# Attention with a low-rank mixer and an MLP on one core: squares, casts and roots of the first five head groups put on other engines and other places in the queues

## The chip, the cores and the metric

The kernel runs on one core of a Trainium2 chip. The metric is the device time of the run in microseconds (us). All times of the profile are from one profiled execution; its clock starts with the first instruction.

## The reference

```python
# q, k, v: (8, 12, 448, 64); g_q, g_k: (64,); U: (448, 32); V: (32, 448)
# w_ch1: (768, 3072); w_ch2: (3072, 768); all float32
rms(x, g) = x / sqrt(mean(x * x, -1) + 1e-6) * g
scores    = rms(q, g_q) @ rms(k, g_k).T / sqrt(64)
attn      = softmax(scores)                       # per batch and head, 448 x 448
x         = (attn @ v), heads side by side        # (8, 448, 768)
u         = x + (x.T @ U @ V).T                   # mixes the 448 tokens through rank 32
out       = u + relu(u @ w_ch1) @ w_ch2           # (8, 448, 768)
```

## The kernel before, in words

**Groups and pairs.** The 96 heads are taken in 24 groups of four heads (three groups to a batch), and each group in two pairs. "Group 0" is the first. A pair is named by batch and number; pairs 0 and 1 belong to group 0, pairs 2 and 3 to group 1, and so on.

**A group's preparation.** Its q, k and v are loaded as float32 (`load_qk`, `load_v`, issued by SyncE). `squares` (line 133) squares q or k, on ScalarE or, where an engine is given, on GpSimd. `sums` (line 158) adds up each row of 64 on VectorE. `roots` (line 161) makes 1/rms from both sums with two short ScalarE instructions (a logarithm, line 165, and an exponential, line 166). `scale` (line 168) multiplies q and k by it and writes bf16 `qn` and `kp`; for most groups both on GpSimd. `turn` (line 339) transposes seven 128x128 blocks on TensorE into PSUM, and `take_q` and `take_k` (lines 347 and 356) copy the result to SBUF as `qT` and `kz`. `values` (line 194) casts v to bf16 in three instructions, one for `va` and two for `vl`. Groups from 6 on are transposed by DMA instead and are not touched by the change. Group 0 is cut into two parts (`PARTS`) so that its chain starts early: `squares_part`, `sums_part`, `scale_part` (line 152).

**A pair's attention.** `Sc(b, pr, r)` for r = 0 to 3 (line 390) makes the transposed scores of two 128-key blocks (for r = 3 of one) in one of two PSUM buffers `sc`, and ScalarE writes their exponentials to `E`. `V(b, pr, half)` (line 401) multiplies `E` by `vl` and `va`; VectorE divides by the sum (`r`, line 419, and `x`, line 420).

**Mixer and MLP.** For batch 0 `prep_u` casts U to `Ub` and `Uz`, `prep_v` casts V, `mix_t0` and `mix` make `uT`, and `mix_rows` (matmul `pm`, line 482, and VectorE's addition, line 490) makes u by rows. `up` (line 496; matmuls line 500, relu line 502) and `down` (line 519; matmuls line 526) are the MLP. `up_part` begins the first two of the 24 columns of `up` ahead of the others.

**The order.** Nothing is scheduled by a tool (`manual_schedule`): each engine runs its instructions in the order in which Python emits them, and semaphores make it wait for others. The front is emitted by the lines from 693 on. After it stands the list `att` of attention steps, each with a cost. For batch 0 it holds `Sc` and, behind each, what the dictionary `extra` names; then come the last V of batch 0, the mixer, and the two `up_part`; then the turning of group 3; then the steps of the later pairs. The loop at the end merges `att` with the list `mlp`: an attention step is taken when the costs of those taken so far are not past `due`. Steps of cost 0 go with the step before them, and `lambda: None` steps only spend cost, so they put off what follows.

**Filler.** `keep_busy(n)` issues n matmuls of 128 columns whose result nobody reads.

```python
        (0, 2): scales(1) + [(0, squares, (2, 1, pool)), (0, keep_busy, (8,))],
...
    squares(1, 0)
    fill_mixer()
    squares(2, 0, nc.gpsimd, ...)
    values(0)
    turn(0, 0)
    keep_busy(14)
```

Of the kernel before, what the change touches and what calls it, by code (L numbers as in the profile page):

```python
# [24 lines left out]
def kernel(  # L25
# [13 lines left out]
    nc = tc.nc  # L39
    B, H, S, D = q.shape  # L40
    dm = H * D
    dh = moe_w_ch1.shape[1]
    rank = moe_U.shape[1]
# [5 lines left out]
    R = S - SM  # L49
# [3 lines left out]
    NW = len(WIN[0])  # L53
    D1 = D + 1
# [26 lines left out]
    NM = 4 * NJ  # L81
# [18 lines left out]
    def by_c(t):  # L100
        return t.rearrange("p (c j) d -> p c j d", c=2)
# [31 lines left out]
    def squares(gi, i, eng=None, sq=None):  # L133
        if sq is None:
            sq = normp.tile([P, 2 * NT, D], FP32, name="sq", tag="sq")
        sqs[(gi, i)] = sq
        if eng is None:
            nc.scalar.activation(sq, staged[gi][i], AF.Square)
        else:
            eng.tensor_mul(sq, staged[gi][i], staged[gi][i])  # L140
# [11 lines left out]
    def scale_part(i, lo, hi, eng):  # L152
        eng.tensor_tensor(
            normed[0][i].rearrange("p j c d -> p c j d")[:, :, lo:hi, :], by_c(staged[0][i])[:, :, lo:hi, :],
            rss[0][:, i].rearrange("p (c j) -> p c j ()", c=2)[:, :, lo:hi, :].to_broadcast([P, 2, hi - lo, D]),
            ALU.mult)

    def sums(gi, i):
        nc.vector.tensor_reduce(ssqs[gi][:, i, :], sqs.pop((gi, i)), AX, ALU.add)  # L159
# [31 lines left out]
                rs[:, c, :2 * NJ].rearrange("p (i t) o -> p i t o", i=2).to_broadcast([P, 2, NJ, D]), ALU.mult)  # L191
            nc.gpsimd.tensor_tensor(rest, src[:, c, 2 * NJ], rs[:, c, 2 * NJ].to_broadcast([P, D]), ALU.mult)

    def values(gi):
        tv, va, vl = staged[gi][2], *normed[gi][2:]
        nc.gpsimd.tensor_copy(va[:, :, :D], tv[:, :NM, :])  # L196
        for e in range(2):
            nc.gpsimd.tensor_copy(vl[e * R:(e + 1) * R, :, e * D1:e * D1 + D], tv[e * R:(e + 1) * R, NM:, :])

    def scale_all(gi):  # L200
        roots(gi)
# [14 lines left out]
    PARTS = ((0, 4), (4, NT))  # L216
# [15 lines left out]
    def keep_busy(n):  # L232
        t = ps.tile([P, P], FP32, name="busy", tag="ps")
        for i in range(n):
            nc.tensor.matmul(t, ident, ident, start=True, stop=True)
# [53 lines left out]
    Ub = consts.tile([P, NJ + 2, rank], BF16)  # L289
    first = xp.tile([P, NW, dm], BF16, name="x", tag="x")  # L290
    Uf = first[:, 2, :2 * (NJ + 2) * rank].bitcast(FP32).rearrange("p (j r) -> p j r", r=rank)
# [26 lines left out]
    Uz = first[:, 0, :NW * P].rearrange("p (j r) -> p j r", r=P)  # L318
    tz = first[:, 1, :]

    def prep_u():
        nc.vector.tensor_copy(Ub, Uf)
        nc.vector.tensor_copy(Uz[:, :, :rank], Uf[:, :NW, :])  # L323

    tb_bufs = [consts.tile([P, 2 * P], BF16, name=f"tb{i}") for i in range(2)]

    def fill_mixer():
        nc.gpsimd.memset(Uz, 0.0)
        for t in tb_bufs:
            nc.gpsimd.memset(t, 0.0)  # L330
# [16 lines left out]
    def take_q(gi, a, scalar=False):  # L347
        qT = q_bufs[gi % 2][:, a]
        dst, src = qT.rearrange("p (j r) -> p j r", r=R), pts[(gi, 0)][:, :, a, :]
        if scalar:  # L350
            nc.scalar.mul(dst, src, gg[:, 0:1])
        else:
            nc.vector.tensor_scalar(dst, src, gg[:, 0:1], None, ALU.mult)
        qk[(gi, a)] = [qT]

    def take_k(gi, a):
        src = pts[(gi, 1)][:, :, a, :]
        kz = kz_bufs[gi % 2][:, a]
        nc.vector.tensor_copy(kz[0:D, :S].rearrange("p (j r) -> p j r", r=R), src[0:D])
        nc.vector.tensor_copy(kz[D:P, S:S + R], src[D:P, 2 * NJ])  # L360
        nc.vector.tensor_copy(kz[D:P, S + R:].rearrange("p (j r) -> p j r", r=R), src[D:P, :2 * NJ])
        qk[(gi, a)].append(kz)
# [183 lines left out]
    att = []  # L546

    def add_att(cost, f, *a):
        att.append((cost, f, a))
# [9 lines left out]
    def V2(i, half):  # L559
        return (0.55, V, (*pairs[i], half))  # L560

    pool = nc.gpsimd

    def scales(gi):
        return [(0, roots, (gi,)), (0, scale, (gi, 0, pool)), (0, scale, (gi, 1, pool))]

    def turns(gi):
# [1 line left out]

    extra = {  # L570
        (0, 0): [(0, keep_busy, (8,))],
        (0, 1): [(0, keep_busy, (8,))],
        (0, 2): scales(1) + [(0, squares, (2, 1, pool)), (0, keep_busy, (8,))],
        (0, 3): [(0, keep_busy, (8,))],
        (1, 1): [V2(0, 0)],
        (1, 2): [(0.4, turn, (1, 0)), (0, take_q, (1, 0)), (0, take_q, (1, 1))],
        (1, 3): [(0.4, turn, (1, 1)), (0, take_k, (1, 0)), V2(0, 1), (0, take_k, (1, 1)), (0, sums, (2, 1)),
                 (0, values, (1,)), (0, load, (4,)), (0, weights, (1,))],
        (2, 1): scales(2) + [(0, weights, (1,)), V2(1, 0)],
        (2, 3): [V2(1, 1), (0, prep_u, ())],  # L580
        (3, 1): [V2(2, 0)],
        (3, 2): turns(2),
        (3, 3): [V2(2, 1), (0, take_k, (2, 1)), (0, squares, (3, 0, pool)), (0, values, (2,)), (0, load, (5,)),
                 (0, weights, (1,)), (0, prep_v, (0, 1)), (0, squares, (3, 1, pool)), (0, weights, (1,))],
        (4, 0): [V2(3, 0)],
        (4, 1): [V2(3, 1), (0, sums, (3, 0))],
        (5, 0): [(0.9, mix_t0, (0, 512))],
# [4 lines left out]
    for i in range(NPAIR):  # L592
        for r in range(4):
            add_att(0.38, Sc, *pairs[i], r)
            att.extend(extra.get((i, r), []))
    att.extend([V2(5, 0), V2(5, 1), (0.39, mix, (0, 2, True)), (0.39, mix, (0, 3, True)), (0.57, up_part, (0, 0, 0, 3)),
                (0.2, mix_t0, (640, dm)), (0.39, mix, (0, 4, True)), (0.57, up_part, (0, 1, 0, 3)),
                (0.39, mix, (0, 5)), (0.19, up_part, (0, 0, 3, 4)), (0.19, up_part, (0, 1, 3, 4)),
                (0, sums, (3, 1))])
    first_done = len(att)  # L600

    att.extend([(0.6, lambda: None, ()), *scales(3)[:2], (0, scale, (3, 1, nc.vector)), (0, values, (3,)), (0.9, lambda: None, ()),
                (0.4, turn, (3, 0)), (0.4, turn, (3, 1)), (0, take_q, (3, 0)), (0, take_q, (3, 1)),
                (0, take_k, (3, 0)), (0, take_k, (3, 1)), (0.3, lambda: None, ())])

    for i, (b, pr) in enumerate(pairs):
        if b == 0:
            continue
        gi, a = divmod(i, 2)
        more = gi + 1 < len(groups)  # L610
        by_dma = gi + 1 >= DMA_FROM
        soon = gi + 2 < len(groups)

        if pr == 0 and b > 1:
            add_att(0.55, V, *pairs[i - 1], 0)
            add_att(0.55, V, *pairs[i - 1], 1)
        add_att(0.38, Sc, b, pr, 0)
        if i == 2 * DMA_FROM - 2:
            add_att(0.0, load, DMA_FROM + 1)
        if a == 0 and by_dma and gi + 1 < len(groups):  # L620
            add_att(0.0, scale_all, gi + 1)
        if b == 1 and pr == 0:
            add_att(0.4, lambda: None)
        if a == 0 and not by_dma:
            add_att(0.0, squares, gi + 1, 0, nc.gpsimd)
            add_att(0.0, squares, gi + 1, 1, nc.gpsimd)
            if gi + 2 >= DMA_FROM:
                add_att(0.0, load, gi + 2)
        add_att(0.38, Sc, b, pr, 1)
        if pr != 0:  # L630
            add_att(0.55, V, *pairs[i - 1], 0)
        if a == 1 and more and not by_dma:
            add_att(0.39, T, gi + 1, 0)
        if a == 1 and soon and gi + 2 >= DMA_FROM:
            add_att(0.0, squares, gi + 2, 0)
            add_att(0.0, squares, gi + 2, 1)
        add_att(0.38, Sc, b, pr, 2)
        if a == 0 and not by_dma:
            add_att(0.0, sums, gi + 1, 0)
            add_att(0.0, sums, gi + 1, 1)  # L640
        if a == 0 and more and by_dma:
            add_att(0.0, turn_dma, gi + 1)
            add_att(0.0, take_dma, gi + 1)
            if gi + 1 == DMA_FROM:
                add_att(0.0, weights, 2)
            if gi + 3 < len(groups):
                add_att(0.0, load, gi + 3)
        if a == 1 and more and not by_dma:
            add_att(0.39, T, gi + 1, 1)
        add_att(0.19, Sc, b, pr, 3)  # L650
        if a == 0 and not by_dma:
            add_att(0.0, scale_all, gi + 1)
        if pr != 0:
            add_att(0.55, V, *pairs[i - 1], 1)
        if a == 1 and soon and gi + 2 >= DMA_FROM:
            add_att(0.0, sums, gi + 2, 0)
            add_att(0.0, sums, gi + 2, 1)
# [35 lines left out]
    a_, b_ = PARTS  # L693
# [11 lines left out]
    roots(0, 1, 2)  # L705
    pg = prep_gains()
    keep_busy(10)
    nc.vector.tensor_copy(gg, pg)
    for part in PARTS:
        scale_part(1, *part, nc.vector)  # L710
    squares(1, 0)
    fill_mixer()
    squares(2, 0, nc.gpsimd,
            uT.rearrange("p k c -> p (k c)")[:, :4 * NT * D].bitcast(FP32).rearrange("p (j d) -> p j d", d=D))
    values(0)
    turn(0, 0)
    keep_busy(14)
    take_q(0, 0, True)
    take_q(0, 1, True)
    squares(1, 1)  # L720
    turn(0, 1)
    take_k(0, 0)
    sums(1, 0)
    sums(1, 1)
    take_k(0, 1)
    sums(2, 0)
    stage_tiles(3)
    load_qk(3, 0)
# [81 lines left out]
```

## Time and profile before

| | |
|---|---|
| time, median of 3 runs | 603.68 us (602.1 to 603.82) |
| profiled execution, its time | 603.46 us |
| its span, first to last instruction | 601.7 us |
| TensorE busy (matmul) | 587.0 us, 98% |
| ScalarE busy | 313.7 us, 52% |
| GpSimd busy | 203.7 us, 34% |
| VectorE busy | 199.1 us, 33% |
| mean granted TensorE clock | 0.996 |

The span is shorter than the execution's time by 1.76 us, which lies around the instructions. A busy share is an average over stages: in the first 60 us the four engines hand work to each other for one group after the other, and later the matmuls of the MLP fill TensorE. PE is the matmul side of TensorE, DVE is VectorE, ACT is ScalarE, POOL is GpSimd, SP is SyncE.

### The profile page before, as it was taken

To read this page: it belongs to the slowest core of one execution; us is meant where nothing else is said; L and a number is where in the kernel's file an instruction comes from. 1 tells how busy PE (TensorE), PEld (TensorE's weight loads), DVE (VectorE), ACT (ScalarE), POOL (GpSimd) and SP (SyncE) were. 2 spreads that over 40 slices of the span, in tenths; PEclk is the share of its full clock that TensorE was granted. 3 is DMA by queue.
4 is the path that set the end of the run, shared out by engine and by line. 5 is a ranking of instruction groups with operands and counts; after the bars stand their busy time and mean duration, and the time that the engine had idled before them with its cause. 6 is when DMAs were issued, how large, how long until landed. Compare 5 with 4: busy or idle time off the path is not lost.

```text
span 601.7 us, 11611 instructions
## 1 busy us (share of the span) xinstructions
PE 587.0 (98%) x4791; PEld 357.6 (59%) x4792; DVE 199.1 (33%) x456; ACT 313.7 (52%) x482; POOL 203.7 (34%) x290
## 2 busy tenths in 40 slices
PE   8788999999999999999999999999999999999996
PEld 7554656655666556655566655665566655655563
DVE  6865544512334212531235220531223310310011
ACT  6865784467453676357654567456763344004300
POOL 7976765344054323425044413524234000000000
PEclk9998999999999999999999999999999999999999
DMA  8999999785369451973274752687025310230022
GB/s 238 198 240 244 258 155 208 133 196 106 91 142 164 130 131 28 190 184 73 67 163 96 185 123 40 139 179 183 10 39 93 80 27 0 53 73 2 0 53 52
DMA packets 118333, 71.73 MB, mean 119 GB/s; under 512 B 80393, under 2 KB 115081, under 8 KB 118281
## 3 DMA queue, kind: packets, MB, share of 16 engines
q1 hardware_dynamic: 108868, 61.56, 45.6%
q0 software_dynamic: 9408, 9.44, 9.6%
q8 instruction: 37, 0.61, 0.4%
q14 instruction: 16, 0.12, 0.1%
q10 hardware_dynamic: 4, 0.00, 0.0%
HBM read 52.20 MB, written 11.01 MB: 105 GB/s over the span
## 4 chain that ended last, share of the span: by engine, by line
PE 87%; DMA 3%; DVE 2%; ACT 1%; issue 1%; POOL 1%; SPq 0%; DVEq 0%; POOLq 0%; ACTq 0%
PE ph L500 35%; PE po L526 34%; PE sc L398 9%; PE pv L416 5%; DMA kz<-kp 2%; PE pv L412 2%; PE pm L485 1%; ACT E L399 1%; DMA out_dram<-ob 1%; PE pu L433 1%; DVE ssq L159 1%; PE pt L344 0%; POOL qn L169 0%; DVE x L323 0%; POOL w2b L282 0%
## 5 line engine op out<-in xcount | busy, mean ns | idle before, releaser
L526 PE MATMUL po<-w2b,hT 128*128 128x384 bf16 x1344 | 241.6, 326 | 0.0
L500 PE MATMUL ph<-uT,w1b 128*128 128x448 bf16 x1140 | 235.6, 354 | 0.0
L399 ACT ACTIVATE E<-sc,gg 128x896 bf16<-128x896 f32 x192 | 172.3, 912 | 111.7 <-PE sc L398 111.6
L526 PEld LDWEIGHTS <-hT 128*128 128x128 bf16 x1344 | 127.1, 98 | 78.6
L502 ACT ACTIVATE hT<-ph 128x448 bf16<-128x448 f32 x190 | 103.0, 545 | 125.6 <-PE ph L500 123.3
L500 PEld LDWEIGHTS <-w1b 128*128 128x128 bf16 x1140 | 108.8, 98 | 96.3 <-issue 1.8
L398 PE MATMUL sc<-qT,kz 128*128 128x448 bf16 x336 | 94.0, 354 | 4.4 <-ACT E L399 3.3
L419 DVE RECIPROCAL r<-pv 128x4 f32<-128x4 f32 x96 | 17.4, 181 | 210.0 <-PE pv L416 209.2
L188 POOL TENSOR_TENSOR qn<-qf,rs 128x384 bf16<-128x384 f32 x36 | 29.9, 831 | 151.8 <-ACT rs L166 135.6
L374 POOL TENSOR_SCALAR qT<-qT,gg 128x896 bf16<-128x896 bf16 x18 | 45.4, 2524 | 84.9 <-DMA qT<-qn 61.8
L534 DVE TENSOR_TENSOR ob<-po,x 128x384 f32<-128x384 f32 x48 | 26.8, 558 | 94.7 <-PE po L526 91.5
L416 PE MATMUL pv<-va,E 128*128 128x65 bf16 x1152 | 57.2, 194 | 0.0
L416 PEld LDWEIGHTS <-E 128*128 128x128 bf16 x1152 | 50.5, 98 | 7.6 <-issue 0.3
L398 PEld LDWEIGHTS <-kz 128*128 128x128 bf16 x336 | 32.0, 98 | 28.3 <-issue 4.2
L159 DVE TENSOR_REDUCE ssq<-sq 128x14 f32<-128x896 f32 x45 | 46.7, 1076 | 0.1
L412 PE MATMUL pv<-vl,E 128*128 128x130 bf16 x192 | 42.1, 219 | 0.1
L420 DVE TENSOR_TENSOR x<-pv,r 128x256 bf16<-128x256 f32 x96 | 40.7, 424 | 3.3
L490 DVE TENSOR_TENSOR x<-pm,x 128x384 bf16<-128x384 f32 x48 | 26.4, 553 | 17.3 <-PE pm L485 15.2
L188 POOL TENSOR_TENSOR kp<-kf,rs 128x384 bf16<-128x384 f32 x36 | 29.9, 830 | 0.0
L412 PEld LDWEIGHTS <-E 128*128 128x128 bf16 x192 | 18.7, 97 | 7.5 <-issue 0.6
L196 POOL CAST va<-vf 128x768 bf16<-128x768 f32 x24 | 19.8, 826 | 0.0
L534 DVE TENSOR_TENSOR ob<-po,u_rest 128x384 f32<-128x384 f32 x8 | 4.5, 558 | 45.9 <-PE po L526 45.9
(91 smaller groups left out, 286.7 us busy)
## 6 DMA issues: line engine op xcount, KB each, us to landing
qf<-in_q_dram SPq DMA_DIRECT2D x23, 448.0 KB, 4.1
kf<-in_k_dram SPq DMA_DIRECT2D x23, 448.0 KB, 5.0
out_dram<-ob SPq DMA_DIRECT2D x50, 192.0 KB, 3.1
vf<-in_v_dram SPq DMA_DIRECT2D x48, 192.0 KB, 5.8
w1b<-in_moe_w_ch_dram POOLq DMA_DIRECT2D x4, 1152.0 KB, 18.6
w2b<-in_moe_w_ch_dram POOLq DMA_DIRECT2D x8, 576.0 KB, 13.1
vf<-in_v_dram SPq DMA_DIRECT2D x48, 32.0 KB, 5.0
out_dram<-ob SPq DMA_DIRECT2D x12, 96.0 KB, 3.2
```

The costliest lines, as they stand in the source:

```text
L159: nc.vector.tensor_reduce(ssqs[gi][:, i, :], sqs.pop((gi, i)), AX, ALU.add)
L188: nc.gpsimd.tensor_tensor(main.rearrange("p (t i) d -> p i t d", i=2), src[:, c, :2 * NJ].rearrange("p (i t) d -> p i t d", i=2), rs[:, c, ...
L374: nc.gpsimd.tensor_scalar(qT, qT, gg[:, 0:1], None, ALU.mult)
L398: nc.tensor.matmul(sc[:, i, :S], kz[:, c:c + P], qT, start=True, stop=True)
L399: nc.scalar.activation(es[(b, pr)][:, 2 * r:2 * r + n, :], sc[:, :n, :S], AF.Exp, scale=scal, bias=bias)
L412: nc.tensor.matmul(pv[:, i].rearrange("p e d -> p (e d)"), E[:, NJ, w:w + P], vl[:, lp, :], start=True, stop=False)
L416: nc.tensor.matmul(pv[:, i, e, :], E[:, e * (NJ + 1) + j, w:w + P], va[:, (first_h + step * e) * NJ + j, :], start=False, stop=(e == 1 and ...
L420: nc.vector.tensor_tensor(xs[b].rearrange("p i (h d) -> p i h d", d=D)[:, 2 * half:2 * half + 2, h0:h0 + step + 1:step, :], pv[:, :, :, :D ...
L500: nc.tensor.matmul(ph, w1b[:, dt, ht * P:(ht + 1) * P], uT[:, dt, off:off + S], start=(dt == 0), stop=(dt == KD - 1))
L502: nc.scalar.activation(hT[:, ht, off:off + S], ph, AF.Relu)
L526: nc.tensor.matmul(po, hT[:, ht, col:col + P], w2b[:, ht, half * HALF:(half + 1) * HALF], start=(ht == 0), stop=(ht == KH - 1))
L534: nc.vector.tensor_tensor(ob[:, h], po, urows(b, col, half), ALU.add)
```

## The change

In the front, k of group 1 is squared by GpSimd instead of ScalarE, and v of group 0 is cast by VectorE instead of GpSimd. The first part of group 0's k is scaled before the gains are copied, and the filler between the two first turnings goes from 14 to 6 matmuls. The roots and scaling of group 1 stand one `Sc` sooner, the sum for k of group 2 stands ahead of the second `take_k` of group 1. U is cast by GpSimd, after the third quarter of w_ch1 is issued, instead of by VectorE. For group 3 the sum for k moves ahead of the last mixer steps, its roots into their middle, and the idle costs ahead of and behind its turning are changed. For groups 4 and 5, roots, scaling and cast of v (`scale_all`) stand ahead of the pair's last `Sc` instead of behind it.

```diff
-    def values(gi):
+    def values(gi, eng=nc.gpsimd):
         tv, va, vl = staged[gi][2], *normed[gi][2:]
-        nc.gpsimd.tensor_copy(va[:, :, :D], tv[:, :NM, :])
+        eng.tensor_copy(va[:, :, :D], tv[:, :NM, :])
         for e in range(2):
-            nc.gpsimd.tensor_copy(vl[e * R:(e + 1) * R, :, e * D1:e * D1 + D], tv[e * R:(e + 1) * R, NM:, :])
+            eng.tensor_copy(vl[e * R:(e + 1) * R, :, e * D1:e * D1 + D], tv[e * R:(e + 1) * R, NM:, :])
...
     def prep_u():
-        nc.vector.tensor_copy(Ub, Uf)
-        nc.vector.tensor_copy(Uz[:, :, :rank], Uf[:, :NW, :])
+        nc.gpsimd.tensor_copy(Ub, Uf)
+        nc.gpsimd.tensor_copy(Uz[:, :, :rank], Uf[:, :NW, :])
...
     extra = {
         (0, 0): [(0, keep_busy, (8,))],
-        (0, 1): [(0, keep_busy, (8,))],
-        (0, 2): scales(1) + [(0, squares, (2, 1, pool)), (0, keep_busy, (8,))],
+        (0, 1): scales(1) + [(0, squares, (2, 1, pool)), (0, keep_busy, (8,))],
+        (0, 2): [(0, keep_busy, (8,))],
...
-        (1, 3): [(0.4, turn, (1, 1)), (0, take_k, (1, 0)), V2(0, 1), (0, take_k, (1, 1)), (0, sums, (2, 1)),
+        (1, 3): [(0.4, turn, (1, 1)), (0, take_k, (1, 0)), V2(0, 1), (0, sums, (2, 1)), (0, take_k, (1, 1)),
                  (0, values, (1,)), (0, load, (4,)), (0, weights, (1,))],
         (2, 1): scales(2) + [(0, weights, (1,)), V2(1, 0)],
-        (2, 3): [V2(1, 1), (0, prep_u, ())],
+        (2, 3): [V2(1, 1)],
...
-                 (0, weights, (1,)), (0, prep_v, (0, 1)), (0, squares, (3, 1, pool)), (0, weights, (1,))],
+                 (0, weights, (1,)), (0, prep_u, ()), (0, prep_v, (0, 1)), (0, squares, (3, 1, pool)), (0, weights, (1,))],
...
-    att.extend([V2(5, 0), V2(5, 1), (0.39, mix, (0, 2, True)), (0.39, mix, (0, 3, True)), (0.57, up_part, (0, 0, 0, 3)),
-                (0.2, mix_t0, (640, dm)), (0.39, mix, (0, 4, True)), (0.57, up_part, (0, 1, 0, 3)),
-                (0.39, mix, (0, 5)), (0.19, up_part, (0, 0, 3, 4)), (0.19, up_part, (0, 1, 3, 4)),
-                (0, sums, (3, 1))])
+    att.extend([V2(5, 0), V2(5, 1), (0, sums, (3, 1)), (0.39, mix, (0, 2, True)), (0.39, mix, (0, 3, True)), (0.57, up_part, (0, 0, 0, 3)),
+                (0.2, mix_t0, (640, dm)), (0.39, mix, (0, 4, True)), (0, roots, (3,)), (0.57, up_part, (0, 1, 0, 3)),
+                (0.39, mix, (0, 5)), (0.19, up_part, (0, 0, 3, 4)), (0.19, up_part, (0, 1, 3, 4))])
...
-    att.extend([(0.6, lambda: None, ()), *scales(3)[:2], (0, scale, (3, 1, nc.vector)), (0, values, (3,)), (0.9, lambda: None, ()),
+    att.extend([*scales(3)[1:2], (0, scale, (3, 1, nc.vector)), (0, values, (3,)), (1.4, lambda: None, ()),
                 (0.4, turn, (3, 0)), (0.4, turn, (3, 1)), (0, take_q, (3, 0)), (0, take_q, (3, 1)),
-                (0, take_k, (3, 0)), (0, take_k, (3, 1)), (0.3, lambda: None, ())])
+                (0, take_k, (3, 0)), (0, take_k, (3, 1)), (0.5, lambda: None, ())])
...
-        add_att(0.19, Sc, b, pr, 3)
         if a == 0 and not by_dma:
             add_att(0.0, scale_all, gi + 1)
+        add_att(0.19, Sc, b, pr, 3)
...
+    scale_part(1, *a_, nc.vector)
     nc.vector.tensor_copy(gg, pg)
-    for part in PARTS:
-        scale_part(1, *part, nc.vector)
+    scale_part(1, *b_, nc.vector)
     squares(1, 0)
+    squares(1, 1, nc.gpsimd)
     fill_mixer()
     squares(2, 0, nc.gpsimd, ...)
-    values(0)
     turn(0, 0)
-    keep_busy(14)
+    keep_busy(6)
     take_q(0, 0, True)
     take_q(0, 1, True)
-    squares(1, 1)
     turn(0, 1)
     take_k(0, 0)
     sums(1, 0)
     sums(1, 1)
     take_k(0, 1)
+    values(0, nc.vector)
     sums(2, 0)
```

## The prediction

> **What bounds the kernel now.** I read the page first, then who waited for whom on TensorE, then the first 60 us in order of time, stretch by stretch.
>
> ```profile
> PE 587.0 (98%) x4791; PEld 357.6 (59%) x4792; DVE 199.1 (33%) x456; ACT 313.7 (52%) x482; POOL 203.7 (34%) x290
> PE   8788999999999999999999999999999999999996
> PEclk9998999999999999999999999999999999999999
> ```
>
> TensorE is the bound, full from slice 5 on. Time can be won or lost only in the first 60 us, where all that the change moves lies, and there the clock was once not fully granted. The waits of TensorE:
>
> ```profile
> PE sc L398 <- ACT E L399: 3.3, 7, 1.1
> PE pt L344 <- POOL qn L169: 2.5, 1, 2.5
> PE sc L398 <- DVE kz L359: 0.9, 2, 0.5
> PE pt L344 <- POOL kp L169: 0.8, 1, 0.8
> ```
>
> The largest single one is the turning of group 3. In order of time, around it (start, length, engine and line):
>
> ```profile
> 44.34 1.09 DVE L169 TENSOR_TENSOR kp<-kf,rs 128x896 bf16<-128x896 f32 x1 [1.70 <-ACT rs L166]
> 44.44 2.54 POOL L169 TENSOR_TENSOR qn<-qf,rs 128x896 bf16<-128x896 f32 x1 [4.04 <-issue]
> 47.03 0.56 PE L344 MATMUL pt<-ident,qn 128*128 128x128 bf16 x7 [2.48 <-POOL qn L169]
> 47.84 2.44 PE L500 MATMUL ph<-uT,w1b 128*128 128x448 bf16 x6
> ```
>
> and the stretches 48 to 49 and 54 to 56 (TensorE, its weight loads, DVE, ACT, POOL, then the granted clock):
>
> ```profile
> 48.00:49.00 1.00, 1.00 (x5) 0.33 (x3) 0.97 (x5) 0.00 (x0) 0.88 (x2) 0.50 1.13 265
> 54.00:56.00 2.00, 2.00 (x12) 1.08 (x11) 0.56 (x1) 1.97 (x4) 0.00 (x0) 1.00 1.14 228
> ```
>
> After 2.48 us of idleness the clock stood at 0.50 from about 47.8 to 51.2: six `ph` matmuls took 2.44 us there and 1.30 us elsewhere. So that one wait costs 2.6 us and then half of 3.4 us. The third thing to see is how VectorE's casts fare beside GpSimd:
>
> ```profile
> 23.61 1.68 POOL L169 TENSOR_TENSOR qn<-qf,rs 128x896 bf16<-128x896 f32 x1 [0.88 <-issue]
> 24.00 1.40 DVE L322 CAST Ub<-x 128x160 bf16<-128x160 f32 x1
> 25.27 1.68 POOL L169 TENSOR_TENSOR kp<-kf,rs 128x896 bf16<-128x896 f32 x1
> 25.32 1.71 DVE L323 CAST x<-x 128x128 bf16<-128x128 f32 x1
> ```
>
> Two casts of 160 and 128 elements last 1.40 and 1.71 us, and each ends 0.1 us after the GpSimd instruction beside it. They were held. At 44.44 it is the other way: GpSimd's `qn`, begun 0.1 us after VectorE's `kp`, takes 2.54 us instead of 1.69. Whoever reads first holds the other off for the whole instruction. The first cast got in between two GpSimd instructions that follow each other without a pause; the second had to let one pass.
>
> **The change part by part**, in the clock of this execution.
>
> *Start, gain 0.44.* 14 filler matmuls take 0.94 us from 9.60; eight fewer at 0.055 us are 0.44. The turning of group 0's k is then due at 9.94. Its `kp`: the first part is ready to start when `rs` ends (8.39) and may be held by GpSimd's `qn` to 8.73, plus 0.55 is 9.27; the second, 0.55 more, 9.82. So `kp` doesn't bind, and the first exponential goes from 12.00 to 11.56. It can, because ScalarE's square of 0.95 us (to 11.80) is gone. That square's data landed at 10.04 (issued 2.26, 7.8 to landing), so GpSimd runs it 10.17 to 11.85 (1.68), then the three memsets (1.03) and the square of group 2's q, to 14.46 instead of 13.44.
>
> *Roots and scaling of group 1 sooner.* VectorE's two sums (2.08) end at 13.53, ScalarE has done two exponentials at 13.47 and waits 0.1; `rs` is there at 14.14 instead of 15.27. GpSimd's `qn` starts at 14.42 instead of 15.40. This would take away the 0.8 us wait for `kp`.
>
> *v of group 0 on VectorE, the dear part.* Behind the second `take_k` (shifted by 0.44) the three casts start at 14.47, where GpSimd begins 5 us of `qn`, `kp` and square with no pause. If the first cast gets in at the boundary (14.46), it takes 0.55 (between the 0.10 that L322 took once released, for 160 of 768 elements, and 1.08 for a reduction that reads 896), so to 15.0; `qn` is held by as much and ends at 16.6; the second cast passes there, `kp` ends at 18.2, the third at 18.3. TensorE's first V, at 16.2 before, needs `vl` and waits until 18.35, and the `Sc` behind it too: the third exponential of the pair starts at 18.35 + 0.53 (V) + 0.55 (scores) = 19.45 instead of 17.47. Behind the casts on VectorE stand the sum of group 2's q (1.08), the division (0.64), two `take_q` (0.81) and a `take_k` (0.38), then scores (0.55): the next pair begins at about 21.6 instead of 20.49, so 1.1 late. Bounds: no hold at all gives 0.8 early (`kp` at 17.8 and no wait for it), a lost boundary 2.7 late. I take 1.1, by L322's row.
>
> On this the Trainium skill speaks against the change: "GPSIMD Engine Reference", section "Key points", has GpSimd share its SBUF interfaces with VectorE, with contention for VectorE instructions in a 2-port mode or with two SBUF inputs. The rows above agree (1.40 us for 160 elements).
>
> *Sum for k of group 2 ahead of `take_k`; U on GpSimd.* ScalarE idled 0.50 at 22.9 for that sum: gain 0.5. Without the casts of U VectorE is free from 24.0 to 27.03, but the turning of group 2 still needs GpSimd's `kp`, so of the 0.40 us that TensorE waited for `kz` at 28.2 and ScalarE's 0.87 behind it I take 0.35 (0 to 0.87). On GpSimd the two casts of U cost about 0.3 each (its casts of 64 to 128 elements take 0.29) and put off `mix_t0`, whose `Uz` is then just in time: 0.2 lost (0 to 0.6). Balance at 36 us: 1.1 - 0.5 - 0.35 + 0.2 = 0.45 late. Loads are issued in the same order; the one that reuses v's tile (21.37) still comes after the casts.
>
> *Group 3.* Its sum for k moves from 41.10 into VectorE's idle 0.89 us at 38.3; roots follow ScalarE's copy (40.13) at 40.15, so `rs` is there at 40.7 instead of 44.30 and GpSimd, done with issuing w2 at 40.4, has `qn` by 43.4 even if held. The turning is due at 44.4. The wait (2.6) and the halved clock (half of 3.4, 1.65 net) go: 4.25 gained.
>
> *Roots of group 4 ahead of the last `Sc`, a new wait.* In the new order TensorE does `pm`, one `Sc` of one block, six `ph`, two blocks of the next pair, and then needs the buffer that the one-block exponential frees. That exponential now stands behind the roots on ScalarE, these behind both sums on VectorE, and these (another move of the merge) behind the addition of this `pm`. From the start of `pm`: addition at 0.36, sums at 0.84 (both 0.48 after in the rows at 51.38 and 51.86), their end at 2.91 (2.07), roots 0.57, exponential to 4.05. TensorE is done with its own at 0.16 + 0.19 + 1.13 + 0.38 = 1.86. It stops for 2.2 us, and the relus behind the roots stop too. Before, the same place (54.40 to 56.45) had no wait. In return `qn` of group 4 is sooner, and the 0.45 us lost at 58.7 (0.32 of it shown as a wait) goes. For group 5 the same move finds VectorE's sums done in time by the rows at 68 to 70: nothing, or a few tenths that the MLP's matmuls hide.
>
> *Sum.* 0.45 - 4.25 + 2.2 - 0.45 = -2.05. From the execution's own 603.46 us (span 601.7 and 1.76 around it) this gives 601.4; I write 601.5. The execution lies 0.2 under the median of the runs shown, 603.68.
>
> **The rivals.**
>
> *The boundary is lost (slower).* My estimates put the cast's start (14.47) and GpSimd's `qn` (14.42) 0.05 us apart, so it may go either way. Then the first cast waits for `qn` (16.1), the second for `kp` (18.2), the third for the square: V starts at 19.9, 1.55 later. TensorE idles from 16 to 19.9, more than the 2.48 us that halved its clock, and what follows is V and turnings at half speed: 1.4 more. 601.5 + 2.95 = 604.4; if the 2.2 us of group 4 then halve the clock as well (1.8), 606.2. It decides whether V starts before 19 us. For it: L323 let a whole instruction pass. Against: L322 did not.
>
> *The clock falls in my own case.* The two new waits of 2.1 and 2.2 us are close to the 2.48 that halved it; one halved stretch costs 1.0 (front, partly under ScalarE) to 1.7: 602.5 to 603.2. The Trainium skill, "TensorE: Matmul & The Clock Gate", section "Part 1: The HAM clock gate", lets the clock fall after an idle window of about 3.4 us; by that neither wait would do it. The row says that 2.48 us were enough.
>
> *The casts of v are not held.* Their tiles are of another shape than U's. Then the pair is 0.8 early instead of 1.1 late: 599.6. Against it: both casts of this kind in the trace were held.
>
> *The roots of group 4 don't wait,* because the sums come sooner than I place them: 601.5 - 2.2 = 599.3.
>
> **How the numbers follow.** My case 0.36, the clock falling in it 0.14, the lost boundary 0.30 (0.18 at 604.4, 0.12 at 606.2), casts not held 0.14, no wait for the roots 0.06. About 0.3% (1.8 us) is what a measurement of this kernel can tell from no change, so faster means under 601.87 and slower over 605.5. My case at 601.5 gives three quarters of its 0.36 to faster, with 0.20 from the last two: 0.47. Slower: 0.12 and a third of the 604.4, as later work could add to it: 0.18. The same: 0.35. The range leaves out the second halved stretch and the very best: 599.5 to 605.0. My case alone: 600.7 to 602.4.
>
> **What would show it.** `va<-vf` and `vl<-vf` casts on VectorE at 14.5 to 18.3 with lengths of 1.6 us, the third ending with GpSimd's `kp`; the first V near 18.4; no wait of `pt` for `qn` in the forties and a clock of 1.00 there; ScalarE idle 1.8 us ahead of a logarithm (line 165) near 53, TensorE idle 2.2 us with it. Casts of 0.3 to 0.6 us, or a clock of 0.50 in 17 to 24 or 52 to 58, would make the prediction wrong.

## The result, and the profile after

| | before | after |
|---|---|---|
| time, median of 20 executions each | 602.82 us (601.7 to 611.17) | 605.54 us (602.31 to 606.3) |
| ratio after / before | | 1.0036, 95% interval 1.0026 to 1.0047 |
| profiled execution, its time | 603.46 us | 602.31 us |
| its span | 601.7 us | 600.5 us |

The kernel is 0.36% slower, some 2.2 us by the ratio (2.7 by the two medians; the kernel before had medians of 603.4 to 603.6 beside the experiments). The profiled execution of after is the fastest of its twenty, so its page shows the change at its best and must not be read as the typical one; two more profiled executions of the same kernel follow below.

First the page of the profiled execution: busy time and instructions of each engine, then TensorE and its granted clock in 40 slices of 15 us.

```profile
PE 585.7 (98%) x4783; PEld 356.6 (59%) x4784; DVE 200.1 (33%) x457; ACT 312.9 (52%) x481; POOL 204.5 (34%) x290
PE   8798999999999999999999999999999999999996
PEclk9899999999999999999999999999999999999999
```

The clock's low slice has moved from the fourth (45 to 60 us) to the second (15 to 30). The waits of TensorE (total, times, longest) say why:

```profile
PE sc L398 <- ACT E L399: 3.8, 5, 2.1
PE pv L412 <- DVE vl L198: 2.2, 1, 2.2
PE sc L398 <- DVE va L196: 0.8, 1, 0.8
PE sc L398 <- POOL qT L374: 0.2, 1, 0.2
```

The wait of 2.5 us for `qn` of group 3 and that of 0.8 us for `kp` are gone from the list. New are 2.2 us for the casts of `vl` and, inside the first line, 2.1 us in one piece. The 0.8 us put down to `va` are probably a wait for ScalarE's exponentials: before, the same scores waited 0.45 us for these, and in `e1_lost` below the same 0.77 us stand under them. In order of time (start, length, engine and line) three places of the same execution: the casts of v in the front, the turning of group 3, and the place ahead of group 4's turning.

```profile
14.32 0.56 DVE L196 CAST va<-vf 128x768 bf16<-128x768 f32 x1
14.39 2.03 POOL L169 TENSOR_TENSOR qn<-qf,rs 128x896 bf16<-128x896 f32 x1
14.79 3.37 DVE L198 CAST vl<-vf 64x128 bf16<-64x128 f32 x2
18.21 0.22 PE L412 MATMUL pv<-vl,E 128*128 128x130 bf16 x1 [2.22 <-DVE vl L198]
...
42.39 2.60 POOL L169 TENSOR_TENSOR qn<-qf,rs 128x896 bf16<-128x896 f32 x1
44.52 1.30 PE L500 MATMUL ph<-uT,w1b 128*128 128x448 bf16 x6
45.66 0.55 PE L344 MATMUL pt<-ident,qn 128*128 128x128 bf16 x7
...
51.98 2.07 DVE L159 TENSOR_REDUCE ssq<-sq 128x14 f32<-128x896 f32 x2
54.09 0.32 ACT L165 ACTIVATE rs<-ssq,eps 128x28 f32<-128x28 f32 x1 [1.68 <-DVE ssq L159]
55.24 0.54 PE L398 MATMUL sc<-qT,kz 128*128 128x448 bf16 x2 [2.06 <-ACT E L399]
```

For comparison the front of the kernel before, with the casts on GpSimd:

```profile
13.49 0.83 POOL L196 CAST va<-vf 128x768 bf16<-128x768 f32 x1
14.26 0.64 POOL L198 CAST vl<-vf 64x128 bf16<-64x128 f32 x2
15.40 1.69 POOL L169 TENSOR_TENSOR qn<-qf,rs 128x896 bf16<-128x896 f32 x1 [0.50 <-DMA kf<-in_k_dram]
16.22 0.22 PE L412 MATMUL pv<-vl,E 128*128 128x130 bf16 x1
```

In the front of the changed kernel the first cast got in 0.08 us ahead of GpSimd's `qn`, which then took 2.03 us instead of 1.69; the two `vl` casts took 3.37 us, each ending just behind a GpSimd instruction, and V started at 18.21 instead of 16.22. The turning of group 3 comes through without a stop and at full clock, six `ph` in 1.30 us instead of 2.44. Ahead of group 4 ScalarE waits for VectorE's sums and TensorE for ScalarE.

Here every wait is where the prediction put it, at 18.2 and at 55.2 us, and the clock fell once, at 19.4, in the front: 602.31 us, next to the case "the clock falls in my own case" (602.5 to 603.2). What the typical execution does had to be found by the experiments.

### The profile page after: what moved, and what is told of

It is laid out like the page before. It is cut to its first block, busy times and chain, and to the rows that moved or that the text cites. A ratio compares the mean times of both kernels' runs of the same rounds, so it can differ in the third digit from the quotient of the medians.

```text
span 600.5 us, 11600 instructions
## 1 busy us (share of the span) xinstructions
PE 585.7 (98%) x4783; PEld 356.6 (59%) x4784; DVE 200.1 (33%) x457; ACT 312.9 (52%) x481; POOL 204.5 (34%) x290
## 4 chain that ended last, share of the span: by engine, by line
PE 91%; DMA 3%; DVE 2%; ACT 2%; issue 0%; SPq 0%; DVEq 0%; ACTq 0%
PE ph L500 36%; PE po L526 34%; PE sc L398 10%; PE pv L416 6%; DMA kz<-kp 2%; PE pv L412 2%; PE pm L485 1%; ACT E L399 1%; PE pt L344 1%; DMA out_dram<-ob 1%; DVE ssq L159 1%; PE pu L433 1%; DMA qf<-in_q_dram 1%; DVE vl L198 1%; PE sc L512 0%
## 5 line engine op out<-in xcount | busy, mean ns | idle before, releaser
L490 DVE TENSOR_TENSOR x<-pm,x 128x384 bf16<-128x384 f32 x48 | 26.4, 554 | 18.3 <-PE pm L485 15.2
```

## The experiments

The times of each run are set against executions of the kernel before on the same chip. Differences in us below are ratio differences times 603, or differences of medians where that is said.

**What does the changed kernel do in other executions?** Two more profiles of it, nothing edited.

Expected of the first:

> The changed kernel once more, for another profiled execution. Theory (most executions lose the boundary): qn of group 1 starts ahead of the first cast of v, V at 19.5 or later, two stretches of half clock, 603.5 to 606. Rival (boundary won in most): V near 18.2 and the time above 604 from something else.

Expected of the second:

> The changed kernel a third time, as the one before. Theory: V at 19.5 or later and 603.5 to 606. Rival: V near 18.2.

Measured: 601.4 and 604.66 us. In the first the load of group 1's k landed as in the profile above (GpSimd's square of it began at 10.14), the first cast started at 14.33, `qn` at 14.39, V at 18.22, the stop ahead of group 4 took 2.06 us, and the clock was at 1.00 until the last 3 us. The time is the forecast, 601.5, to the tenth; neither what was expected of this run nor its rival, which had a time above 604, came. In the second, in order of time:

```profile
11.54 1.68 POOL L140 TENSOR_TENSOR sq<-kf 128x896 f32<-128x896 f32 x1 [2.99 <-DMA kf<-in_k_dram]
15.29 0.96 DVE L196 CAST va<-vf 128x768 bf16<-128x768 f32 x1
15.78 2.00 POOL L169 TENSOR_TENSOR qn<-qf,rs 128x896 bf16<-128x896 f32 x1
16.16 3.35 DVE L198 CAST vl<-vf 64x128 bf16<-64x128 f32 x2
19.57 0.27 PE L412 MATMUL pv<-vl,E 128*128 128x130 bf16 x1 [2.61 <-DVE vl L198]
```

and the stretches of 1 us (TensorE, weight loads, VectorE, ScalarE, GpSimd, then the granted clock):

```profile
18.00:19.00 1.00, 0.00 (x0) 0.00 (x0) 1.00 (x1) 0.38 (x1) 1.00 (x1) 0.66 1.05 396
24.00:25.00 1.00, 1.00 (x5) 0.34 (x3) 0.93 (x4) 0.06 (x1) 0.00 (x0) 0.50 0.79 179
```

The load landed 1.4 us later, at 11.41 instead of 10.01. GpSimd's square moved by as much, the second sum, the roots and the casts by about 1.0; the first cast still got in ahead of `qn`, but V came at 19.57, and the clock stood at 0.50 from 18.3 to 25.2, two stretches of 3.4 us. So the expectation was right on V, clock and time, and wrong on how: not the boundary but the landing. One halved stretch is 0.0028 of the mean clock of a 600-us run (half of 3.41 us), and up to 0.0022 more went at the end of the kernel, where TensorE runs out of work (`look_a`, without a fall before 596.9 us, shows 0.998). Of the twenty executions of after, the profiled one shows a mean clock of 0.996 and one more 0.995, which is one stretch each. 12 lie at 0.993 or 0.994, which is two stretches as here, and 6 lower still, at 0.989 to 0.992, with up to three or four. Where the stretches of these executions lie is not on record.

**The boundary forced either way.** `e1_lost` puts one more VectorE copy ahead of the casts; `e2_first` puts a small GpSimd copy, which waits for VectorE's last copy of `kz`, ahead of `qn`. Both copies go to a tile that is not yet in use.

```diff
 # e1_lost
     take_k(0, 1)
+    nc.vector.tensor_copy(tz[0:D, :S]..., pts[(0, 1)][0:D, :, 1, :])
     values(0, nc.vector)
 # e2_first
-        (0, 1): scales(1) + [...]
+        (0, 1): [(0, nc.gpsimd.tensor_copy, (tz[D:P, :R], kz_bufs[0][D:P, 1, 2 * S - R:]))] + scales(1) + [...]
```

> One more copy of 0.38 us on VectorE ahead of the three casts of group 0's v, so that GpSimd's qn is sure to start first. Theory (who reads first at 14.4 us decides, and most executions of the changed kernel are on the losing side): the first cast is held to the end of qn, the three casts end near 20, the first V of the profile starts at 19.8 to 20.3 instead of 18.2, a clock of 0.50 follows, and every time lies at 603.8 to 606.3. Rival (the changed kernel's times spread because of the clock alone, wherever it falls; the boundary is always won): the extra copy costs its 0.4 us and the times spread as before, 602.5 to 606.5, with V at 18.6.

> A GpSimd copy of 64 by 64 elements ahead of qn, which waits for the last copy of kz on VectorE: the first cast of v is sure to start before qn. Theory: all executions are like the profiled one of the changed kernel, V at 18.2 to 18.5, the clock at 0.50 once between 20 and 24 us, times 602.0 to 603.2, none above 604. Rival (the clock alone): the same spread as the changed kernel, 602.3 to 606.3, with most above 605.

Measured: lost, 604.98 us median, ratio 1.0031 (1.0014 to 1.0048), as the change itself; in its profile the first cast took 1.61 us, V came at 19.62, and the clock was at 0.50 from 18.7 to 25.5. Its times lie between 602.27 and 607.14, wider than the 603.8 to 606.3 expected. Won, 601.87 us, ratio 0.9984 (0.9966 to 1.0002). The two differ by 2.8 us by the ratios, so "the clock alone" is out. That is more than the boundary, though: in the profile of `e2_first` the second cast got in ahead of `qn` as well, in 0.26 us, and V came at 17.1. The won times still spread from 599.96 to 604.89, wider than expected: there was no fall of the clock in front, and yet a halved stretch from 53.9 to 57.4, behind the stop of 2.06 us.

**The two late parts undone, alone and together.** In `e3_v_pool` GpSimd casts group 0's v where it did before; in `e4_roots_back` the roots of groups 4 and 5 stand behind the last `Sc` again; `e5_both_back` has both.

```diff
 # e3_v_pool, e5_both_back
     squares(2, 0, nc.gpsimd, ...)
+    values(0)
     turn(0, 0)
 ...
-    values(0, nc.vector)
 # e4_roots_back, e5_both_back
+        add_att(0.19, Sc, b, pr, 3)
         if a == 0 and not by_dma:
             add_att(0.0, scale_all, gi + 1)
-        add_att(0.19, Sc, b, pr, 3)
```

> The change with the cast of group 0's v left on GpSimd, where it stood before. Theory: no cast to hold, V at about 16, no wait of 2.2 us and no halved clock in front; against the profiled execution of the change (602.3) 1.1 us of delay and 1.0 us of clock go, so 600.2, and the times lie within 1 us of each other (599.7 to 601.2). Rival (the spread comes from the stop ahead of group 4's roots at 53 to 55 us and its clock): the times still spread over 2 to 4 us, 600 to 604, and a clock of 0.50 shows near 55 to 58 in some of them.

> The change with roots, scaling and cast of v of groups 4 and 5 behind the pair's last scores again. Theory (boundary and clock in front, and a second halving at group 4's stop where the front was late): the stop of 2.2 us at 53 goes and the 0.45 us at 58.7 comes back, so executions with a won boundary come to 600.6 and those with a lost one to 602.2 to 602.8; nothing above 603.5. Rival (the stop at group 4 makes all of the spread): all times between 600.2 and 601.2. Rival (the front makes all of it): the spread stays 4 us wide, 600.5 to 604.5.

> The change without its two late parts: the cast of group 0's v on GpSimd as before, and roots, scaling and cast of v of groups 4 and 5 behind the pair's last scores. Theory (each stop of 2 us or more costs itself and, in about half of the executions, half of a stretch of 3.4 us at half clock): from the run with v on GpSimd alone (median 601.6) the 2.06 us of the stop and half of 1.7 us go and 0.45 us come back, so 599.1, with no clock of 0.50 in the profile. Rival (what spreads the times is the landing of group 1's k, which came at 11.65 us in one profile and at 10.04 in another): the median falls by 1.6 at most, and the times still spread over 4 us.

Measured: 601.59 us, ratio 0.9974 (0.996 to 0.9989); 602.92 us, 0.9993 (0.998 to 1.0006); 601.63 us, 0.9992 (0.9968 to 1.0015). Each alone turns slower into no worse than before; the gain of both together did not come. The change (1.0036) against `e3_v_pool` (0.9974) puts 3.7 us on the casts of v. The profile of `e3_v_pool` shows two causes of spread at once: k landed at 11.62, so the roots were at 15.16 instead of 13.98, and its stop at 53 to 55 us was followed by a halved stretch from 55.9 to 59.3. `e4_roots_back`, without that stop, still spreads over 3.0 us, to 604.48, where its theory had nothing above 603.5. In `e5_both_back` seven of twelve times lie between 600.4 and 601.6, five between 603.1 and 606.9. Its one profile, 601.63, has no fall of the clock and does not explain the upper five. Their mean clocks, 0.992 to 0.995 against 0.998 to 1.000 for the seven, say that they lost at least one stretch, most of them two or more; what started these stays open.

**The casts out of GpSimd's way.** `e7_clear_roots_back` makes GpSimd wait for the last cast before `qn` (and has the roots of groups 4 and 5 back).

```diff
-        (0, 1): scales(1) + [...]
+        (0, 1): [(0, nc.gpsimd.tensor_copy, (tz[R:P, :D], vl_bufs[0][R:P, 1, D1:D1 + D]))] + scales(1) + [...]
```

> A GpSimd copy of 64 by 64 elements ahead of qn of group 1, which waits for the last of the three casts of v on VectorE, and groups 4 and 5 as before. Theory (casts cost little where nothing of GpSimd stands beside them): the three casts take 0.56, 0.26 and 0.26 us and end near 15.6, V does not wait for them, qn starts near 15.8, the turning of group 1 waits about 1 us for kp, and the time is 599.0 to 600.0. Rival (casts of v on VectorE are dear in any place): V later than 17 and 600.5 to 602.

```profile
15.55 0.96 DVE L196 CAST va<-vf 128x768 bf16<-128x768 f32 x1
16.43 0.47 DVE L198 CAST vl<-vf 64x128 bf16<-64x128 f32 x2
17.37 1.69 POOL L169 TENSOR_TENSOR qn<-qf,rs 128x896 bf16<-128x896 f32 x1
```

With GpSimd idle the two `vl` casts take 0.21 and 0.23 us; beside it they took 1.62 to 1.71. So the hold is shown, and its size for these casts: 1.4 to 1.5 us each. The `va` cast, 0.96 us here, began while GpSimd still squared (until 16.10) and ended 0.42 us after. The time, 602.11 us, ratio 0.9979 (0.996 to 0.9998), is 2 us over what was expected: k landed at 11.67 in the profile, V came at 17.07 and `qn` at 17.37 instead of 15.8. That is close to the rival's numbers, but not by its cause, since the casts were short; what the time would be with an early landing is not shown.

**The clock held by filler.**

```diff
 # e8_filler
-        (1, 1): [V2(0, 0)],
+        (1, 1): [(0, keep_busy, (26,)), V2(0, 0)],
 ...
+        if i == 7:
+            add_att(0.0, keep_busy, 24)
         add_att(0.38, Sc, b, pr, 1)
 # e9_before_filler, on the kernel before
-                (0.4, turn, (3, 0)), (0.4, turn, (3, 1)), ...
+                (0, keep_busy, (28,)), (0.4, turn, (3, 0)), (0.4, turn, (3, 1)), ...
```

> The change with filler matmuls in the two places where TensorE now stops: 26 ahead of the first V, 24 ahead of the scores that wait for the roots of group 4. They run while TensorE would stand still, so no wait gets shorter, but the clock has no idle window. Theory (the clock takes what the waits alone do not explain): no clock of 0.50, median 602.0 to 603.5 instead of 605.5, and a spread of 2 us at most. Rival (the waits themselves are that long): 605 to 606, as without filler.

> The kernel before with 28 filler matmuls ahead of the turning of group 3, where TensorE stood still for 2.48 us. Theory (its times are of two kinds, with and without the halved stretch, 1.7 us apart): no clock of 0.50 near 48 to 51, all times between 601.2 and 602.7, median 601.9 against 603.45. Rival (the spread of the kernel before has another cause, such as the landing of the first loads): median and spread as before, 603.4 and 3 us.

Measured: 604.09 us, ratio 1.0009 (0.9994 to 1.0024), against 1.0036 without filler, which puts some 1.6 us of the excess on the clock. The median lies between theory and rival, and the spread is 3.7 us. The filler ahead of V was too short: it ended at 17.6, TensorE then idled 2.10 us and the clock fell once, from 20.2 to 23.7; at group 4 only 0.72 us were left and nothing fell. This profile also shows the boundary lost without help: k landed by 9.7, `qn` started at 14.31, the first cast at 14.52, V at 19.74. On the kernel before, filler changed nothing that can be measured, 603.33 us, ratio 1.0000 (0.9972 to 1.0027). The interval is as wide as the 1.65 us looked for, so the times neither show nor refute that its two kinds come from that stretch. The recorded clocks say more: of the 35 executions of the kernel before on that chip, 15 have a mean clock of 0.998 or more and a median of 602.1 us, 15 one of 0.995 to 0.997 and 603.7, which are 1.6 us apart, as one halved stretch would make them. With filler 8 of 12 have 0.999 or 1.000, but their median is 602.8; where the 0.7 us went stays open.

**Group 3's part alone, on the kernel before** (`e10_before_group3`: the three edits from `V2(5, 0)` to the idle cost behind the turning, as in the change).

> The kernel before with the group 3 part of the change alone (sum ahead of the last mixer steps, roots in their middle, the idle costs moved). Theory (the wait of 2.48 us and the half stretch of clock behind it are worth 4.25 us where both showed, and the clock's share of 1.65 only in part of the executions): no wait of the turning for qn in the forties, no clock of 0.50 there, median 599.5 to 600.5 against about 603.4. Rival (what is gained there is lost again where group 6's qT comes, near 96 us): a wait of 2 us or more there and 601.5 to 603.

Measured: 601.07 us, ratio 0.9967 (0.994 to 0.9994), some 2.0 us faster. Its waits of TensorE:

```profile
PE sc L398 <- POOL qT L374: 1.3, 1, 1.3
PE pt L344 <- ACT E L399: 1.1, 1, 1.1
```

The wait of 2.48 us and the halved stretch (1.65) are gone from this profile, 4.1 us. Of these TensorE loses 0.8 again at the next turning (1.15 instead of 0.32, behind ScalarE's exponentials) and 1.3 at 94 us, where it now comes too early for group 6's `qT`, which reaches it by DMA transposes and had made nobody wait before. That leaves 2.0, and theory and rival each hold in part. That it is the measured gain to the tenth is in part luck: the interval of the ratio is 0.4 to 3.6 us, the two profiled executions differ by 2.9 us (603.46 and 600.57), and not every execution of the kernel before has the halved stretch (43 of 108 on the four chips show a clock of 0.998 or more).

**The square of group 1's k back on ScalarE.** Three versions: on top of the two late parts undone (`e11_k_scalar`), alone (`e12_k_only`), and with the roots of groups 4 and 5 as changed (`e13_stop_only`, `e11_k_scalar` with the stop).

```diff
 # all three; e11_k_scalar and e13_stop_only also cast v by GpSimd, e11_k_scalar also has the roots behind Sc
-    squares(1, 1, nc.gpsimd)
 ...
     take_q(0, 1, True)
+    squares(1, 1)
     turn(0, 1)
```

> As the run without the two late parts, and the square of group 1's k on ScalarE again, so that GpSimd no longer has to wait for the landing of that load. Theory (with k on GpSimd a late landing delays four instructions behind it; it came between 9.5 and 11.7 us in the profiles): the first exponential goes back to about 12, qn of group 1 starts at 15 to 15.5 whatever the landing, times closer together, 599 to 601, median 600. Rival (the landing does not matter for the end): 601.6 as with k on GpSimd.

> The change with the square of group 1's k on ScalarE again, all else as changed: v of group 0 cast by VectorE, roots of group 4 ahead of the last scores. Theory (the casts beside GpSimd's qn are the dear part, whatever lands when): qn starts near 14.2 and the first cast near 14.5, so the boundary is lost in nearly all executions, V near 19.5, 604 to 606. Rival (the landing of k in GpSimd's queue is the dear part): 601.5 to 603.

> The best version so far (k of group 1 squared by ScalarE, v of group 0 cast by GpSimd, groups 4 and 5 as before; median 600.2) with the roots, scaling and cast of v of groups 4 and 5 ahead of the pair's last scores, as in the change. Theory (the stop costs 2.06 us, half of 1.7 us of clock on average, and gives 0.45 back): 602.2 to 602.9. Rival (what is lost at 53 us comes back where TensorE otherwise waits 1.9 us for group 6's qT at 94): 600.5 to 601.3.

Measured: `e11_k_scalar` 600.2 us, ratio 0.9946 (0.9922 to 0.997), the best version, faster than both kernels; its profiled execution has a span of 597.6 us at a clock of 1.00, `qn` of group 1 starts at 14.51 and V does not wait. `e12_k_only` 605.4 us, ratio 1.003 (1.0009 to 1.005). `e13_stop_only` 600.6 us, ratio 0.9959 (0.9946 to 0.9973). The profile of `e12_k_only` is the lost boundary in full:

```profile
14.43 1.69 POOL L169 TENSOR_TENSOR qn<-qf,rs 128x896 bf16<-128x896 f32 x1 [0.42 <-DMA kf<-in_k_dram]
14.64 1.90 DVE L196 CAST va<-vf 128x768 bf16<-128x768 f32 x1
16.46 3.35 DVE L198 CAST vl<-vf 64x128 bf16<-64x128 f32 x2
19.86 0.27 PE L412 MATMUL pv<-vl,E 128*128 128x130 bf16 x1 [3.54 <-DVE vl L198]
```

`e12_k_only` and `e13_stop_only` differ only in which engine casts group 0's v, and at which place of its queue: 605.4 against 600.6 us, 4.3 us by the ratios. V starts at 19.86 instead of 15.95, the next pair's first exponential at 24.90 instead of 20.89: the 4 us are there at 25 us, and the front's clock is in them (0.50 from 17.5 to 24.3). With the casts on VectorE it makes no difference that can be told whether k's square is on ScalarE (1.0030) or on GpSimd (1.0036). So the casts are the dear part, whatever lands when; the change against `e3_v_pool`, 3.7 us, says the same with k on GpSimd. With the casts on GpSimd the place of k's square may count: `e5_both_back` and `e11_k_scalar` differ in it alone, 1.4 us by the medians and 2.8 by the ratios, but on two chips and with intervals that just touch.

The stop for group 4 is the surprise the other way: `e13_stop_only` against `e11_k_scalar` is 0.4 us by the medians, 0.8 by the ratios. The waits of TensorE of `e11_k_scalar`:

```profile
PE sc L398 <- POOL qT L374: 1.9, 1, 1.9
PE pt L344 <- ACT E L399: 1.1, 1, 1.1
```

and the first two of `e13_stop_only`, which has neither of those two:

```profile
PE sc L398 <- ACT E L399: 4.7, 7, 2.1
PE busy L235 <- POOL ident masks.py:199: 1.4, 1, 1.4
```

A stop of 2.06 us took the place of one of 1.1 and of the wait for `qT` at 94 us. My reading, argued from these lists and not shown by a run of its own, is that where the front is early enough TensorE would have stood still there anyway. The profile of `e13_stop_only` is also 1.3 us later at its second pair (20.89 against 19.59) and waits 0.87 us near 35 us for `Vm`, whose load landed late, so its stop is not all that filled the place. In the change, whose front is 4 us late where the casts come late, that slack is used up (0.2 to 0.3 us of it are left in the profiles of after, `look_b` and `e12_k_only`), and undoing the stop brought 2.6 us (`e4_roots_back`).

## Why the prediction was wrong

The step that failed is the term for the casts of v: 1.1 us, with 0.30 for the lost boundary. Measured, the casts cost 3.7 to 4.3 us on average.

**Group 3, minus 4.25.** The mechanism held (no wait, clock at 1.00 in the forties), the size did not: 2.0 us. The sum stopped at 60 us. I looked for what is late next at group 4's turning, and not at 94 us, where the next group's `qT` comes at its own pace. And the 1.65 us of clock are the loss of an execution like the profiled one; 43 of the 108 did not show it.

**v of group 0 on VectorE, the step that failed.** The mechanism is as predicted: casts held for a whole GpSimd instruction, each ending 0.1 us after it. The Trainium skill, "GPSIMD Engine Reference", section "Key points", spoke against the change here, and the trace agrees: 1.62 to 1.71 us beside GpSimd, 0.21 to 0.23 without. The price of my own case holds: in `look_a` the second pair begins at 21.67 instead of 20.49, 1.2 us late (the terms of that sum add up to 21.76, not to the 21.6 that I wrote). The rival's price was right too: 1.1 for my case and 2.95 more make 4.05, measured 4.3. Wrong was which of the two is the usual case. I set the cast (14.47) against `qn` (14.42) by one execution's landing of k at 10.04 and called the 0.05 us between them a coin. But the change itself hung GpSimd's queue on that landing, and in the profiled executions with GpSimd squaring k the square began at 9.6 to 11.8 us. My case needs a window: with the landing at 10.0, three of ten profiles, the cast wins by 0.06 to 0.11 us and V comes at 18.2. With an earlier one (9.56, `e8_filler`) `qn` waits only for the roots and starts first, V at 19.74; with a later one (11.41, `look_b`) everything is late, V at 19.57. In `e12_k_only`, where ScalarE squares k, `qn` started 0.13 us after the roots and 0.2 us ahead of the cast, V at 19.86. Where V came at 19.5 or later two stretches in a row were halved, or one with filler. That the 19 executions of after that have no profile missed the window is inferred: they took 603.8 us or more, and each shows a lower clock than the profiled one. The rival deserved the larger chance, not 0.30.

**The clock.** I gave the fall a chance of its own and took "close to 2.48" as doubtful. The stop of 2.06 us ahead of group 4 halved the clock in `e2_first`, `e3_v_pool` and `e12_k_only`, and not in after, `look_a`, `look_b`, `e1_lost` and `e13_stop_only`. In each execution falls and rises lie whole multiples of 3.41 us apart: 3.41 or 6.83 for a halved stretch, 13.65 from the first rise to the fall in after and `look_b`, 40.96 between the two falls (17.5 and 58.5) of `e12_k_only`. The first rise comes anywhere from 4.2 to 7.3 us. The Trainium skill, "TensorE: Matmul & The Clock Gate", section "Part 1: The HAM clock gate", says that the activity window of 3413 ns runs freely and does not start with the kernel. The traces agree. Laying windows of 3.41 us back from each fall, every one with 2.06 us or more of TensorE idleness halved the clock (2.06 to 2.64 in the first 60 us). One with 1.84 did too (`e12_k_only`, 14.1 to 17.5), and those with up to 1.91 (`look_a`, `e11_k_scalar`, `e13_stop_only`) did not, so the border is not sharp in these rows. A stop of 2.1 us is thus halved or not by where the windows fall, which the profile of one execution cannot say. The same section lets the clock fall after an idle window of about 3.4 us. Here some 60% of one was enough.

**Stop for the roots, plus 2.2, minus 0.45 at 58.7.** Place and length were right, 2.06 us at 55.2. Its price depends on what is around it: 0.4 us in an early front (`e13_stop_only` against `e11_k_scalar`), 2.6 in the change's late one (`e4_roots_back`), and with v on GpSimd and k's square too nothing that can be told (`e3_v_pool` 0.9974, `e5_both_back` 0.9992).

**Start gain 0.44, group 1's roots, U.** The first exponential came at 11.41 instead of 12.00 (11.56 predicted; group 0's roots were 0.15 sooner in this execution), `rs` at 13.98 for 14.14 predicted, and group 2's preparation had no new wait. These hold, and with group 3's part they are what `e11_k_scalar` keeps: 3.3 us under the kernel before.

**The sum again.** All but the casts of v and the move of k is worth 2.5 us (`e13_stop_only`); my terms without the 1.1 for the casts make 3.15. The casts cost 4.3, where I took 1.1. 4.3 less 2.5 is 1.8, and the change is 2.2 us slower; the 0.4 left is the move of k, less than these runs can tell from nothing.

## What to carry to other kernels

Where two instructions of VectorE and GpSimd are ready within 0.1 us of each other and the first one holds the other off for its whole length, find out what their starts hang on before giving chances; if it is the landing of a load, one profile shows one landing, and the order must be fixed by the program or priced at its dear side. Give VectorE casts to do where GpSimd is idle, not where it runs instructions without a pause. A gain early in the kernel counts only up to the next thing that comes at its own pace: follow it to the next transfer that TensorE will be too early for.

## What the runs showed of the hardware that was not expected

- The load of group 1's k, issued near 2.3 us, landed between 9.45 and 11.67 us in the profiles of the changed kernel and its variants, none of which touches what is issued ahead of it.
- Idleness of 2.06 to 2.64 us inside one window of 3.41 us always halved the clock of the stretch behind it, 1.84 us did once, and up to 1.91 us otherwise did not. Where a stop of 2.6 us or more ran across the border of a window, two stretches in a row were halved (18.3 to 25.2, 17.5 to 24.3, 18.7 to 25.5); a stop of 2.22 us that a border split into 0.7 and 1.5 halved none (`look_a`).
- GpSimd's instruction gave way as well: `qn` took 2.00 to 2.05 us instead of 1.69 when a cast had begun 0.06 to 0.5 us before it.
